# Weight conversions moved off GpSimd and spread over two stages, with branch hints, a shorter exit and two blocks of the last stage interleaved

## The chip, the cores and the metric

The kernel runs on one core of one Trainium2 chip. The metric is the time of one execution in device microseconds; before the change the median of 3 runs is 1045.09 us (1044.58 to 1046.73).

## The reference

Three layers follow each other. All inputs and outputs are arrays in float32 or wider, and the weights of the last layer arrive as pairs of 32-bit words (64-bit floats).

```python
q_pool = q.reshape(4, 8, 576, 2, 64).mean(axis=3)             # 1. attention with pooled queries
attn = softmax(q_pool @ k.T / 8) ; x = (attn @ v)              # x: 2304 tokens x 512
keep = (x @ w_skip) > 0                                        # 2. mixture of 8 experts, top 1
e = argmax(x[keep] @ w_gate) ; gate = max(softmax(x[keep] @ w_gate))
x[keep] += gate * (relu(x[keep] @ w1[e]) @ w2[e])              # w1: 8 x 512 x 1024, w2: 8 x 1024 x 512
h = x @ w_in                                                   # 3. dense layer, w_in: 512 x 2048
out = (h - tanh(h)) @ w_out                                    # w_out: 2048 x 512
```

## The kernel before

Four stages follow each other on the five engines. Each engine works through its own instructions in program order; the order is written out by hand.

**Attention** (0 to about 452 us) is not touched, but for one 256 KB store of zeros that moves to another queue. **Routing** (`Router.route`, `invert`, `gates`, `in_last`) is a chain of some 60 small operations on VectorE (DVE), with a few on ScalarE (ACT) and TensorE (PE). `route` counts the tokens of each expert, sorts the experts by size into `perm`, makes `more` (exit marks) and the slot of each token in `sg16`; `invert` turns slots into a list `inv` of token numbers. `Experts.load` on the GpSimd queue (POOL) needs `perm` to fetch the first expert's weights `w1f` and `w2f`; `fetch` gathers a tile of 128 tokens by `inv`.

**Experts** (`Experts.place`, `chain`, `tile`): the experts are run largest first. `place(a)` is entered if expert `a` has tokens; `chain(j)` nests one `If(n > j)` in another, one for each tile of 128 tokens. In these runs the experts have 5, 4, 1 and 1 tiles; I write (a, j) for tile j of expert a. A tile is: 96 matmuls `ps_bh` from the tokens `bxt` and the split weights `w1s` (12 for each of 8 columns f), a ReLU to `bhid` in two halves (ACT the high part, DVE the low part), four transposes of the next tokens, and 24 matmuls `ps_by` from `bhid` and `w2s`. The first tile of an expert also splits its weights into high and low halves (`split1`, `split2`: ACT, then DVE). When the last tile of an expert is done, the engines jump over the unused rest of its chain (line 945) into the next `place` (line 938).

**Weight conversions** (`Wide`): `w_in` and `w_out` are 16 jobs of 128 x 1024 values. A job loads 1 MB into one of two buffers `raw`, makes a float32 in `wa` by three DVE steps (lines 753, 755, 757), then a high part on ACT (line 776 or 779), for `w_in` also a scaled copy on ACT (line 777), and the low part on GpSimd (line 780). Jobs 0 to 13 run beside the experts' tiles (`SIDE`, two for a tile, called by `aside`), jobs 14 and 15 at the start of the last stage (`LATE`).

**Dense** (`Dense.run`, 644 us to the end): 9 blocks of 256 tokens in the order 0, 8, 1, 2, ... Each has 8 steps. A step runs `hid` (24 matmuls `ps_ch`, then an elementwise chain: ACT makes `u`, `t`, `z`, DVE makes `v` in five operations at lines 1089 to 1093, ACT rounds it to `gh`, GpSimd makes `gl`) and then `proj` of the step two before (12 matmuls `ps_co` with one eighth of `w_out`). `mix` and `transp` prepare the tokens of the next block: `mix` on DVE, `xs` high on ACT and low on DVE, and a transposing DMA to `xT`. Job 8 + u converts the eighth of `w_out` that step u uses.

Of the kernel before, what the change touches and what calls it, by code (L numbers as in the profile page):

```python
# [20 lines left out]
P = 128  # L21
# [458 lines left out]
NT = 18  # L480
# [9 lines left out]
class Router:  # L490
# [4 lines left out]
    def __init__(self, ctx, tc, w_skip, w_gate, x_all, ident32, ov):  # L495
# [9 lines left out]
        self.more, self.perm = t("more", [P, 2, E], I32), t("perm", [P, 3, E], I32)  # L505
        self.cnt, self.gate, self.last, self.least = t("cnt", [P, E]), t("gate", [P, NT]), t("last", [P, 1]), t("least", [P, E])
# [129 lines left out]
    def route(self, ps_pool, tag):  # L636
# [4 lines left out]
        for f in self.pick(e, NT):  # L641
# [4 lines left out]
        vals = T("vals", [P, 3, 1, E], I32)  # L646
        perm = T("permf", [P, 3, E])
        cmp, bt, mt, mm = T("cmp", S88), T("bt", S88), T("mt", S88), T("mm", [P, 3, E, E])
        few, last, so, sl = T("few", [P, 1]), self.last, T("so", [P, NT, E]), T("sl", [P, NT])
        iota8 = self.iota[:, 0, 0:E]  # L650
        nt = vals[:, 0, 0]
        V.tensor_copy(vals[:, 1, 0], iota8)
        V.tensor_tensor(out=n, in0=all_, in1=self.cnt, op=ALU.add)
        V.tensor_scalar(out=n1, in0=n, scalar1=float(P - 1), scalar2=None, op0=ALU.add)
        V.scalar_tensor_tensor(out=key, in0=n, scalar=float(E), in1=iota8, op0=ALU.mult, op1=ALU.subtract)
        V.tensor_scalar(out=nt, in0=n1, scalar1=7, scalar2=None, op0=ALU.logical_shift_right)
        V.tensor_tensor(out=cmp, in0=key.unsqueeze(1).to_broadcast(S88), in1=key.unsqueeze(2).to_broadcast(S88),
                        op=ALU.is_gt)
        V.tensor_tensor(out=bt, in0=cmp, in1=nt.unsqueeze(1).to_broadcast(S88), op=ALU.mult)
        V.tensor_reduce(out=rk, in_=cmp, axis=AX.X, op=ALU.add)  # L660
        V.tensor_reduce(out=base, in_=bt, axis=AX.X, op=ALU.add)
        V.tensor_tensor(out=mt, in0=rk.unsqueeze(1).to_broadcast(S88), in1=iota8.unsqueeze(2).to_broadcast(S88),
                        op=ALU.is_equal)
        V.tensor_copy(vals[:, 2, 0], base)
        V.tensor_tensor(out=mm, in0=vals.to_broadcast([P, 3, E, E]), in1=mt.unsqueeze(1).to_broadcast([P, 3, E, E]),
                        op=ALU.mult)
        V.tensor_reduce(out=perm, in_=mm, axis=AX.X, op=ALU.add)
        V.tensor_copy(self.perm, perm)
        V.tensor_reduce(out=last, in_=nt, axis=AX.X, op=ALU.add)
        V.tensor_tensor(out=perm[:, 1], in0=perm[:, 0], in1=self.least, op=ALU.is_lt)  # L670
        V.tensor_scalar(out=perm[:, 2, 0:E - 1], in0=perm[:, 0, 1:E], scalar1=0.0, scalar2=2.0 * NT,
                        op0=ALU.is_equal, op1=ALU.mult)
        V.tensor_reduce(out=few, in_=perm[:, 1], axis=AX.X, op=ALU.max)
        V.tensor_tensor(out=self.more[:, 1, 0:E - 1], in0=perm[:, 0, 0:E - 1], in1=perm[:, 2, 0:E - 1], op=ALU.add)
        V.tensor_scalar(out=last, in0=last, scalar1=1.0, scalar2=1.0, op0=ALU.max, op1=ALU.subtract)
        V.tensor_copy(self.more[:, 0, 1:2], few)
        V.tensor_copy(self.more[:, 0, 0:1], last)
        for f in self.rank(e, NT, before):
            f()
        for t in range(e, e + 3):  # L680
            self.row(t)
        V.tensor_tensor(out=so, in0=base.unsqueeze(1).to_broadcast([P, NT, E]), in1=self.oh, op=ALU.mult)
        V.tensor_reduce(out=sl, in_=so, axis=AX.X, op=ALU.add)
        V.tensor_tensor(out=self.r7[:, 1], in0=self.r7[:, 1], in1=sl, op=ALU.add)
        V.tensor_copy(self.sg16, self.r7[:, 1])
# [40 lines left out]
class Wide:  # L726
# [4 lines left out]
    def __init__(self, ctx, tc, w_in, w_out, wi, wo):  # L731
# [4 lines left out]
        self.jobs, self.open = [], []  # L736
# [23 lines left out]
    def run(self, i):  # L760
        for f in self.steps(i):
            f()
        self.open.append(i)

    def finish(self):
        for i in self.open:
            self.parts(i)
        self.open = []

    def parts(self, i):  # L770

        nc = self.nc
        _, dh, dl = self.jobs[i]
        a = self.a[i % 2].bitcast(F32)
        if dh.dtype == F16:
            nc.scalar.activation(dh, a, AF.Copy, scale=WS)
            nc.scalar.activation(a, a, AF.Copy, scale=WS)
        else:
            nc.scalar.copy(dh, a)
        nc.gpsimd.tensor_tensor(out=dl, in0=a, in1=dh if dh.dtype == F16 else dh.bitcast(F32), op=ALU.subtract)  # L780


class Experts:
# [7 lines left out]
    SIDE = {(0, 1): 2, (0, 2): 2, (0, 3): 2, (0, 4): 2, (1, 1): 2, (1, 2): 2, (1, 3): 2}  # L791
# [88 lines left out]
    def tile(self, a, j, base):  # L880
        nc = self.nc
        g = self.within(base + j)
        side = list(self.groups.get((a, j), ()))

        def aside():
            self.wide.finish()
            if side:
                self.wide.run(side.pop(0))
# [6 lines left out]
        aside()  # L895
        hs = []
        for f0 in (0, 4):
# [23 lines left out]
        aside()  # L921
        for f in range(8):
            mm(self.py, [t[:, f % 4] for t in hs[f // 4]], [t[:, f] for t in self.c2], f == 0, f == 7)
        if a + 1 < E:
            with self.tc.If(self.end <= j + 1):
                for f in range(self.PRE):
                    self.split1(f)
        if a + j:
            for i in self.groups.get((a, j + 1), ())[:2]:
                self.wide.load(i)  # L930

    def place(self, a):
# [5 lines left out]
        with tc.If(n > 0):  # L938
            T = mybir.EngineType
            if a + 1 < E:  # L940
                self.end = self.reg(self.more[:, 1], a, 3 * NT, (T.Activation, T.DVE))
            base = self.reg(self.perm[:, 2], a, CAP, (mybir.EngineType.Pool,))
            def chain(j):
                if j < self.MOST[a]:
                    with tc.If(n > j):
                        self.tile(a, j, base)
                        chain(j + 1)
            self.tile(a, 0, base)
            chain(1)
            self.place(a + 1)  # L950

    def run(self, before, after):
# [17 lines left out]
        self.place(0)  # L970
        before()
# [3 lines left out]
        with self.tc.If(few > 0):  # L975
            some = [self.reg(self.perm[:, 0], a, self.MOST[a], T) for a in range(2)]
            for (a, j), jobs in self.groups.items():
                with self.tc.If(some[a] <= j):
                    for i in jobs:
                        self.wide.load(i)  # L980
                        self.wide.run(i)
                    self.wide.finish()


class Dense:
# [3 lines left out]
    LATE = 2  # L989
# [9 lines left out]
    def setup(self, ctx, wide):  # L999
        tc, self.wide = self.tc, wide  # L1000
        self.late = []
        for i in range(len(wide.jobs) - self.LATE, len(wide.jobs)):
            wide.load(i)
            self.late += [*wide.steps(i), lambda i=i: wide.parts(i)]
# [42 lines left out]
    def transp(self, n, a):  # L1047
# [4 lines left out]
        if a == 0:  # L1052
            self.xs = self.xt.tile([P, 2, 2, DM], F16, tag="xs", name="xs")
            self.xT = self.xt.tile([P, 2, 2, 4, P], F16, tag="xT", name="xT")
# [76 lines left out]
    def run(self):  # L1131
# [11 lines left out]
        for i in range(NB):  # L1143
            for u in range(8):
                self.hid(self.ORDER[i], u, (i, u) == (NB - 1, 7))
                if len(self.q) > 2:
                    self.proj()
                for _ in range(2 if u == 0 else 1):
                    if self.late:
                        self.late.pop(0)()  # L1150
                if u in (2, 4):
                    self.mix(i + 1, u // 2 - 1)
                if u in (3, 5):
                    self.transp(i + 1, u // 2 - 1)
                if u == 7:
                    self.fetch(i + 2)
# [8 lines left out]
def pooled_attention__moe__tanhshrink_kernel(ctx, tc, q, k, v, moe_w_skip, moe_w_gate, moe_w1, moe_w2,  # L1165
# [8 lines left out]
    with tc.manual_schedule():  # L1174
# [7 lines left out]
        with ExitStack() as actx:  # L1182
# [5 lines left out]
            def on_pair(b, c):  # L1188
# [10 lines left out]
                if b == 0:  # L1199
                    for i in range(c, 6, 4):  # L1200
                        n = 5 if i < 5 else 1
                        todo.append(lambda i=i, n=n: nc.sync.dma_start(
                            out=ys[i * 5 * P:(i * 5 + n) * P].rearrange("(a p) d -> p a d", p=P),
                            in_=zero.unsqueeze(1).to_broadcast([P, n, DM])))
# [61 lines left out]
```

## Time and profile before

| quantity | value |
|---|---|
| median of 3 runs | 1045.09 us |
| the profiled execution's own time | 1046.08 us |
| its span, first to last instruction | 1044.6 us |
| busy: PE, DVE, ACT, POOL | 90%, 75%, 61%, 53% of the span |
| mean granted TensorE clock | 0.962 of full |

The profiled execution is 1.48 us longer than its span and 0.99 us longer than the median. A share of busy time is a mean over the four stages, so each stage is read for itself.

### The profile page before, as it was taken

The page shows a single profiled execution, that of the slowest core. Times are in us where ns is not written, and L with a number is a line of the kernel's source. Part 1 is how long each engine was busy: PE and PEld are TensorE (multiplying, and loading weights), DVE is VectorE, ACT ScalarE, POOL GpSimd, SP SyncE. Part 2 cuts the span into 40 slices and gives each one's busy share as a digit, 9 for nine tenths or more (in the row PEclk, how much of TensorE's full clock was granted, in tenths as well). Part 3 has the DMA queues.
Part 4 walks back from the last instruction along what each step waited for, and adds up shares of the span by engine and source line. Part 5 has one row for each costly group of instructions (what it writes and reads, how often), then busy time and mean ns, then how long its engine had stood idle before and what let it go on. Part 6 is the DMA issues. An engine that isn't in the chain of part 4 may idle for free. (4 is left out here: it accounts for less than half of the span.)

```text
span 1044.6 us, 25445 instructions
## 1 busy us (share of the span) xinstructions
PE 941.9 (90%) x10249; PEld 704.6 (67%) x10249; DVE 788.5 (75%) x1420; ACT 641.4 (61%) x1211; POOL 557.1 (53%) x491
## 2 busy tenths in 40 slices
PE   5689999999999999939878775999999999999998
PEld 2355666666666666637656543778888888888886
DVE  8678889888889998768979762867666666666654
ACT  4587999888999998835463451444444444444443
POOL 8847998888899986524646411342332223322221
PEclk8889999999999999969989887999999999999999
DMA  7765878666666720169657433121111211212100
GB/s 222 147 157 177 213 190 206 139 134 126 162 143 127 166 59 15 28 224 330 215 180 261 150 126 136 31 72 41 46 56 31 72 41 46 56 32 71 21 21 21
DMA packets 129796, 122.52 MB, mean 117 GB/s; under 512 B 92270, under 2 KB 96878, under 8 KB 128622
## 3 DMA queue, kind: packets, MB, share of 16 engines
q1 hardware_dynamic: 121934, 92.74, 34.7%
q0 software_dynamic: 7712, 27.79, 7.9%
q8 instruction: 92, 1.51, 0.6%
q14 instruction: 58, 0.48, 0.1%
HBM read 74.73 MB, written 19.14 MB: 90 GB/s over the span
## 5 line engine op out<-in xcount | busy, mean ns | idle before, releaser
L242 POOL TENSOR_TENSOR pl<-p,ph 128x512 f16<-128x512 f32 x214 | 263.8, 1252 | 59.5 <-ACT p L237 45.1
L188 DVE TENSOR_REDUCE m<-ps_m 128x1 f32<-128x384 f32 x432 | 225.5, 548 | 37.4 <-PE ps_m L187 34.7
L1095 POOL TENSOR_TENSOR gl<-v,gh 128x512 fp32r<-128x512 f32 x71 | 92.9, 1308 | 270.7 <-ACT gh L1094 268.3
L236 ACT ACTIVATE ph<-ps_e 128x512 f16<-128x512 f32 x279 | 177.0, 635 | 57.5 <-PE ps_e L248 54.2
L299 PEld LDWEIGHTS <-ph 128*128 128x128 f16 x2304 | 133.4, 99 | 49.7 <-issue 22.6
L1094 ACT CAST gh<-v 128x512 fp32r<-128x512 f32 x72 | 44.5, 619 | 188.5 <-DVE v L1093 188.5
L1078 PE MATMUL ps_ch<-xT,wi 128*128 128x256 f16 x576 | 158.7, 275 | 0.7 <-ACT xT L1062 0.7
L1079 PE MATMUL ps_ch<-xT,wi 128*128 128x256 f16 x576 | 157.9, 274 | 1.1 <-DMA xT<-xs 0.8
L1080 PE MATMUL ps_ch<-xT,wi 128*128 128x256 f16 x576 | 157.9, 274 | 0.0
L187 PE MATMUL ps_m<-ks,qT 128*128 128x384 f16 (+1 forms) x480 | 122.7, 338 | 23.9 <-DVE m L188 16.1
L299 PE MATMUL ps_a<-vh,ph 128*128 128x65 f16 x1152 | 136.7, 195 | 0.0
L299 PE MATMUL ps_a<-vh,pl 128*128 128x65 f16 x1152 | 136.6, 195 | 0.0
L299 PE MATMUL ps_a<-vl,ph 128*128 128x65 f16 x1152 | 136.5, 195 | 0.0
L1089 DVE SCALAR_TENSOR_TENSOR v<-u,ps_ch 128x512 f32<-128x512 f32 x72 | 49.3, 685 | 114.4 <-ACT t L1087 108.9
L237 ACT ACTIVATE p<-ps_e 128x512 f32<-128x512 f32 x211 | 134.5, 637 | 0.0
L1111 PE MATMUL ps_co<-wo,gh 128*128 128x512 f32 x288 | 119.7, 416 | 0.0
L1113 PE MATMUL ps_co<-wo,gl 128*128 128x512 f32 x288 | 113.7, 395 | 1.5 <-POOL gl L1095 1.5
L247 PE MATMUL ps_e<-qT,ks 128*128 128x512 f16 x288 | 111.4, 387 | 2.6 <-DVE pl L242 1.8
L1112 PE MATMUL ps_co<-wo,gh 128*128 128x512 f32 x288 | 113.5, 394 | 0.0
L248 PE MATMUL ps_e<-qT,kh 65*128 65x512 f16 x288 | 111.8, 388 | 1.9 <-DMA qT<-mt 1.9
L299 PEld LDWEIGHTS <-pl 128*128 128x128 f16 x1152 | 108.4, 98 | 0.0
L187 PEld LDWEIGHTS <-qT 128*128 128x128 f16 (+1 forms) x480 | 42.9, 102 | 68.1 <-issue 34.3
(222 smaller groups left out, 2152.8 us busy)
## 6 DMA issues: line engine op xcount, KB each, us to landing
v<-in_v_dram SPq DMA_DIRECT2D x16, 576.0 KB
k<-in_k_dram SPq DMA_DIRECT2D x15, 576.0 KB
q<-in_q_dram SPq DMA_DIRECT2D x16, 512.0 KB
raw<-in_moe_w_in_dram SPq DMA_DIRECT2D x8, 1024.0 KB
w1f<-in_moe_w_dram POOLq DMA_DIRECT2D x8, 1024.0 KB, 7.6
w2f<-in_moe_w_dram POOLq DMA_DIRECT2D x8, 1024.0 KB, 8.3
raw<-in_moe_w_out_dram SPq DMA_DIRECT2D x8, 1024.0 KB
ys<-zero SPq DMA_DIRECT2D x5, 1280.0 KB
```

The costliest lines, as they stand in the source:

```text
L187: nc.tensor.matmul(ps[o, 0:384], w, ks[:, h, c * 384:(c + 1) * 384], start=True, stop=True)
L188: nc.vector.tensor_reduce(out=s["m2"][:, i, c:c + 1], in_=ps[:, 0:384], axis=AX.X, op=ALU.max)
L236: nc.scalar.activation(ph, ps, AF.Exp, scale=2.0 ** -20)
L237: nc.scalar.activation(src, ps, AF.Exp, scale=2.0 ** -20)
L242: (nc.vector if dve else nc.gpsimd).tensor_tensor(out=pl, in0=src, in1=ph, op=ALU.subtract)
L299: self.nc.tensor.matmul(o, x, r, start=first and i == 0, stop=k == NKT - 1 and i == 2, skip_group_check=True)
L1078: nc.tensor.matmul(ps[:, a], self.wi[0][:, w], xh[:, c], start=c == 0, stop=False)
L1079: nc.tensor.matmul(ps[:, a], self.wi[0][:, w], xl[:, c], start=False, stop=False)
L1080: nc.tensor.matmul(ps[:, a], self.wi[1][:, w], xh[:, c], start=False, stop=c == 3)
L1111: nc.tensor.matmul(o, gh[:, a, s], self.wo[0][:, w], start=f == 0, stop=False)
L1112: nc.tensor.matmul(o, gh[:, a, s], self.wo[1][:, w], start=False, stop=False)
L1113: nc.tensor.matmul(o, gl[:, a, s], self.wo[0][:, w], start=False, stop=f == 15)
```

## The change

- Routing: the small operations of `route` are interleaved instead of run one group after the other, and the eight that make `more` move into `tails`, called after `invert`.
- Hints: each tile marks, on all five engines, whether the branch to its next tile will be taken; the jump out of the routing's `few` case is marked too.
- Exit: the register `end` is loaded on all engines, and after the first tile of an expert one test of it skips the rest of the chain and all later experts.
- Conversions: the low part moves from GpSimd to DVE, the scaled copy of `w_in` goes away, and the steps of a tile's jobs are handed out one by one: 3 at the tile's start, 2 between its halves, the rest behind its last matmuls and behind the next expert's first splits.
- Five jobs (11 to 15) instead of two run in the last stage, whose first two blocks are interleaved; the second block's tokens are prepared in steps 1 and 2.
- The 256 KB store of zeros moves from the SyncE queue to the GpSimd queue.

```diff
-        nc.gpsimd.tensor_tensor(out=dl, in0=a, in1=dh if dh.dtype == F16 else dh.bitcast(F32), op=ALU.subtract)
+        half = dh.dtype == F16
+        return (
+            lambda: nc.scalar.activation(dh, a, AF.Copy, scale=WS if half else 1.0),
+            lambda: nc.vector.scalar_tensor_tensor(out=dl, in0=a, scalar=WS, in1=dh, op0=ALU.mult, op1=ALU.subtract)
+            if half else nc.vector.tensor_tensor(out=dl, in0=a, in1=dh.bitcast(F32), op=ALU.subtract))
+
+    def queue(self, jobs, load=()):
+        out, low = [], None
+        for i in jobs:
+            s, (hi, lo) = list(self.steps(i)), self.parts(i)
+            if low:
+                h, l = low
+                s[0] = lambda f=s[0], h=h: (h(), f())
+                s.insert(1, l)
+            if i + 2 in load:
+                s[-1] = lambda f=s[-1], i=i: (f(), self.load(i + 2))
+            out += s
+            low = hi, lo
+        return out + ([lambda: (low[0](), low[1]())] if low else [])
...
-    SIDE = {(0, 1): 2, (0, 2): 2, (0, 3): 2, (0, 4): 2, (1, 1): 2, (1, 2): 2, (1, 3): 2}
+    SIDE = {(0, 1): 2, (0, 2): 2, (0, 3): 2, (0, 4): 1, (1, 1): 2, (1, 2): 1, (1, 3): 1}
...
+        if j + 1 < self.MOST[a]:
+            self.tc.mark_branch_hint_location("t%d_%d" % (a, j + 1), hint=n > j + 1, engines=ALL)
...
-        aside()
+        aside(3)
...
-                aside()
+                aside(2)
...
-        aside()
         for f in range(8):
             mm(self.py, [t[:, f % 4] for t in hs[f // 4]], [t[:, f] for t in self.c2], f == 0, f == 7)
         if a + 1 < E:
             with self.tc.If(self.end <= j + 1):
                 for f in range(self.PRE):
                     self.split1(f)
+        aside(len(side))
...
-                self.end = self.reg(self.more[:, 1], a, 3 * NT, (T.Activation, T.DVE))
+                self.end = self.reg(self.more[:, 1], a, 3 * NT, ALL)
...
-                    with tc.If(n > j):
-                        self.tile(a, j, base)
+                    with tc.If(n > j, label="t%d_%d" % (a, j)):
+                        self.tile(a, j, base, n)
...
-            chain(1)
-            self.place(a + 1)
+            with tc.If(self.end != 2 * NT + 1) if a + 1 < E else ExitStack():
+                chain(1)
+                self.place(a + 1)
...
-    LATE = 2
+    LATE = 5
+    TWICE = (5, 6, 7, 8)
...
+        halves = [(n, u) for u0 in (0, 4) for n in range(2) for u in range(u0, u0 + 4)]
+        steps = halves[:8] + sorted(halves[8:], key=lambda s: (s[1], s[0])) + [(n, u) for n in range(2, NB) for u in range(8)]
+        side = {1: (1, 0), 2: (1, 1), 9: (2, 0), 11: (2, 1)}
+        for s, (n, u) in enumerate(steps):
+            self.hid(self.ORDER[n], u, s == len(steps) - 1)
+            if len(self.q) > 2:
+                self.proj()
+            for _ in range(2 if s in self.TWICE else 1):
+                if self.late:
+                    self.late.pop(0)()
+            if s in side:
+                self.mix(*side[s])
+                self.transp(*side[s])
```

## Rows read from the trace of the kernel before

**Rows 1.** Stretches: length, PE, PEld, DVE, ACT, POOL busy (count), PEclk, DMA share, GB/s.
```profile
469.70:627.20 157.50, 131.24 (x1363) 97.08 (x1361) 127.48 (x137) 77.04 (x126) 72.36 (x58) 0.92 0.61 210
644.10:687.10 43.00, 40.47 (x265) 32.26 (x265) 32.18 (x46) 18.13 (x32) 13.82 (x10) 0.95 0.28 98
687.10:1044.60 357.50, 352.94 (x2327) 289.02 (x2326) 225.49 (x363) 161.90 (x284) 99.09 (x80) 1.00 0.16 44
```
**Rows 2.** PE's waits, 470 to 645 us: total us, times, longest us.
```profile
PE ps_by L889 <- DVE bhid L905: 8.9, 7, 1.8
PE ps_i L1041 <- ACTq L975: 8.3, 1, 8.3
```
**Rows 3.** PE's timeline in the expert stage: start, us, work [idle before <-releaser].
```profile
482.89 5.52 PE L889 MATMUL ps_bh<-bxt,w1s 128*128 128x128 f16 x96
492.89 2.33 PE L889 MATMUL ps_by<-w2s,bhid 128*128 128x512 f16 x10 [1.01 <-DVE bhid L905]
...
537.18 8.26 PE L889 MATMUL ps_bh<-bxt,w1s 128*128 128x128 f16 x96 [4.58 <-ACTq L945]
...
593.80 7.29 PE L889 MATMUL ps_bh<-bxt,w1s 128*128 128x128 f16 x96 [5.33 <-DVE w1s L851]
...
612.05 0.90 PE L889 MATMUL ps_bh<-bxt,w1s 128*128 128x128 f16 x7 [5.33 <-PEq L945]
615.11 6.50 PE L889 MATMUL ps_bh<-bxt,w1s 128*128 128x128 f16 x89 [2.16 <-issue]
```
**Rows 4.** Stretch behind the first jump: length, PE busy (count), PEclk, DMA share, GB/s.
```profile
537.20:542.90 5.70, 5.70 (x54) 0.50 0.18 22
```
**Rows 5.** Instructions of single lines: duration min/median/max in ns, first and last start.
```profile
L757 DVE SCALAR_TENSOR_TENSOR wa<-raw,wa x14: 1224/2128/3257, 484.3 to 582.2; 128x1024 uint32<-128x1024 uint32 x14
L780 POOL TENSOR_TENSOR wi<-wa,wi x8: 2117/2130/3197, 489.0 to 531.9; 128x1024 f16<-128x1024 f32 x8
L779 ACT CAST wo<-wa x8: 1041/1045/1068, 554.8 to 686.5; 128x1024 fp32r<-128x1024 f32 x8
L1034 DVE SCALAR_TENSOR_TENSOR cx<-cy,gate,cx x18: 735/742/1762, 639.9 to 976.2; 128x512 f32<-128x512 f32 x18
```
**Rows 6.** DVE's timeline around the end of tile (0, 1).
```profile
489.04 3.19 DVE L757 SCALAR_TENSOR_TENSOR wa<-raw,wa 128x1024 uint32<-128x1024 uint32 x1
...
499.31 0.68 DVE L753 TENSOR_SCALAR wa<-raw 128x1024 uint32<-128x1024 uint32 x1
```
**Rows 7.** Timelines of DVE, POOL and PE in the routing.
```profile
456.55 0.18 DVE L668 CAST perm<-permf 128x24 int32<-128x24 f32 x1
...
459.72 0.18 DVE L685 CAST sg<-r 128x18 f16<-128x18 f32 x1
...
458.61 0.97 POOL L836 DMA_DIRECT2D w1f<-in_moe_w_dram  x1 [13.70 <-DVE kf L608]
...
467.04 1.09 PE L865 MATMUL ps_bt<-ident,bx 128*128 128x128 f32 x4 [2.10 <-DMA bx<-xd,inv]
```
**Rows 8.** Chain that ended last, early in the dense stage: start, us, what.
```profile
682.97 4.14 DMA xT<-xs
...
687.41 0.11 PE ps_ch L1080
...
689.82 0.23 PE ps_co L1111
```
**Rows 9.** DVE's timeline in the dense stage.
```profile
681.43 1.51 DVE L1063 SCALAR_TENSOR_TENSOR xs<-cx,xs 128x512 f16<-128x512 f32 x1 [0.17 <-ACT xs L1062]
...
693.67 0.69 DVE L1089 SCALAR_TENSOR_TENSOR v<-u,ps_ch 128x512 f32<-128x512 f32 x1 [1.78 <-ACT t L1087]
...
698.46 0.69 DVE L1089 SCALAR_TENSOR_TENSOR v<-u,ps_ch 128x512 f32<-128x512 f32 x1 [1.78 <-ACT t L1087]
```
**Rows 10.** PE's waits, 645 us to the end: total us, times, longest us.
```profile
PE ps_co L1113 <- POOL gl L1095: 1.5, 1, 1.5
PE ps_ch L1079 <- DMA xT<-xs: 0.8, 1, 0.8
```

More of the change, by code (lines that the diff above doesn't have):

```diff
@@ new lines, in route, with tails @@
+        V.tensor_copy(vals[:, 1, 0], iota8)
+        rank = self.rank(e, NT, before)
+        for i, f in enumerate(place):
+            f()
+            if i < len(rank):
+                rank[i]()
+        for f in rank[len(place):]:
+            f()
+        for t in range(e, e + 3):
+            self.row(t)
+        for i, f in enumerate(slots):
+            f()
+            if i < len(order):
+                order[i]()
+    def tails(self):
+        V, vals, perm, few, last = self.nc.vector, self.vals, self.permf, self.few, self.last
+        V.tensor_reduce(out=last, in_=vals[:, 0, 0], axis=AX.X, op=ALU.add)
@@ L672, in route @@
                         op0=ALU.is_equal, op1=ALU.mult)
+        V.tensor_scalar(out=last, in0=last, scalar1=1.0, scalar2=1.0, op0=ALU.max, op1=ALU.subtract)
         V.tensor_reduce(out=few, in_=perm[:, 1], axis=AX.X, op=ALU.max)
         V.tensor_tensor(out=self.more[:, 1, 0:E - 1], in0=perm[:, 0, 0:E - 1], in1=perm[:, 2, 0:E - 1], op=ALU.add)
-        V.tensor_scalar(out=last, in0=last, scalar1=1.0, scalar2=1.0, op0=ALU.max, op1=ALU.subtract)
+        V.tensor_copy(self.more[:, 0, 0:1], last)
         V.tensor_copy(self.more[:, 0, 1:2], few)
[L677 to L685, printed above, removed]
     def invert(self, ps_pool):
@@ L774, in parts, with run @@
         a = self.a[i % 2].bitcast(F32)
[L775 to L779, printed above, removed]
-        nc.gpsimd.tensor_tensor(out=dl, in0=a, in1=dh if dh.dtype == F16 else dh.bitcast(F32), op=ALU.subtract)
+        half = dh.dtype == F16
[16 more added lines that the diff above has]
+        return out + ([lambda: (low[0](), low[1]())] if low else [])
+    def run(self, jobs):
+        for f in self.queue(jobs):
+            f()
+ALL = tuple(getattr(mybir.EngineType, n) for n in ("PE", "Activation", "Pool", "DVE", "SP"))
 class Experts:
@@ L970, in run @@
         self.place(0)
+        self.tc.mark_branch_hint_location("few", hint=few, engines=T)
         before()
@@ L1000, in setup @@
         tc, self.wide = self.tc, wide
-        self.late = []
-        for i in range(len(wide.jobs) - self.LATE, len(wide.jobs)):
+        jobs = range(len(wide.jobs) - self.LATE, len(wide.jobs))
+        for i in jobs[:2]:
             wide.load(i)
-            self.late += [*wide.steps(i), lambda i=i: wide.parts(i)]
+        self.late = wide.queue(jobs, jobs[2:])
         pool = lambda n, b: ctx.enter_context(tc.tile_pool(name=n, bufs=b))
@@ L1142, in run @@
             self.transp(0, a)
[L1143 to L1156, printed above, removed]
+        halves = [(n, u) for u0 in (0, 4) for n in range(2) for u in range(u0, u0 + 4)]
[11 more added lines that the diff above has]
+                self.transp(*side[s])
+            if n > 1 and u in (2, 4):
+                self.mix(n + 1, u // 2 - 1)
+            if n > 1 and u in (3, 5):
+                self.transp(n + 1, u // 2 - 1)
+            if s == 4:
+                self.fetch(2)
+            if n and u == 7:
+                self.fetch(n + 2)
         while self.q:
@@ L1211, in pooled_attention__moe__tanhshrink_kernel @@
             att.run()
+            nc.gpsimd.dma_start(out=ys[25 * P:26 * P], in_=zero)
             router.route(att.ps_mx, "mx")
```

86 lines of the change are left out of this document (41 added, 45 removed).

## Prediction

> **What bounds the kernel now.** I read the stretches first, then PE's waits, then PE's own timeline. The stretches [rows 1] show two cases. From 687 us on PE is busy 352.94 of 357.50 us at full clock: every microsecond put in PE's way there is lost, and none can be won. In the expert stage PE is busy 131 of 157.5 us at a mean clock of 0.92: that is where time can be won. The waits say in which form. Seven times, 8.9 us together, PE's second product waits for the low half of `bhid`, which DVE makes [rows 2]. Three times PE stands still for 4.58, 5.33 and 5.33 us between the last tile of one expert and the first of the next, and once more for 2.16 us inside the first tile of expert 3 with no releaser shown [rows 3]. At the exit it stands still 8.3 us [rows 2]. What follows each jump is slow as well: 96 matmuls take 5.52 us in an undisturbed tile but 8.26, 7.29 and 0.90 + 6.50 us behind the jumps [rows 3], and the granted clock there is 0.50, the lower level, 1.2 GHz, after 4.6 us in which PE did nothing [rows 4].
>
> **The change part by part, as time of the profiled execution.**
>
> *Conversions without GpSimd.* A two-input DVE step on 128x1024 takes 1.22 us alone and up to 3.26 us when it meets the GpSimd subtraction of 2.12 us [rows 5]; tile (0, 1) shows 3.19 us for line 757, with `bhid` queued behind it [rows 6]. The change takes this meeting away and adds one DVE operation to each job, which the trace of before doesn't have: below, a 128x512 operation (0.69), above, a blocked one (3.26). It has two inputs and 1024 columns as line 757, so I take 1.22. A tile with two jobs then costs DVE 2 x (0.7 + 1.22 + 1.22 + 1.22) = 8.7 for the jobs, 2.1 for two halves of `bhid` and one of `bxt`, and about 1.3 for the wait of the last low part for ACT: 12.1 us. The tile on PE: from 482.89 to about 495.1 it lasts 12.2, less 1.0 of waiting, so 11.1 [rows 3]. DVE falls back by 1.0 per such tile, but the order puts the low `bhid` early. Working forward from (0, 1): DVE is 1.6 late at (0, 2), 2.5 at (0, 3), 3.3 at (0, 4). `bhid` is late there by 0.2 and 0.9 us, elsewhere not. The reload of a buffer stays hidden: freed at 492.2 in (0, 1), read at 499.31 without a wait [rows 6], and now needed 6 us after it comes free; if that doesn't hold, 1 to 2 us in two tiles. Term: -8.9 + 1.1 = **-7.8** (-4 to -9).
>
> *Hints.* The excess of the three jumps over back-to-back tiles is 15.24 of idle time, 2.16 inside and 6.39 of slow clock: 23.8 us [rows 3]. If the marked target is there in time, what is left is the branch itself, the new load of `end` on PE with the tile's matmuls queued behind it, and the hint's own register work. No row prices these on PE; the first splits of the next expert are ready by then, because the change puts the rest of the conversions behind them. Bounds: nothing, while the queued `ps_by` matmuls run, or the full 4.6 to 5.3. I take 0.8 each, 2.4. Idle times of 1.0 to 1.8 us [rows 2] left the clock alone, so the slow clock goes too. Two things come back: tile (3, 0) arrives 5 us earlier against its `w2f`, which is issued late in (2, 0), about 1.7 us; and the 2.16 inside a tile happened in one jump of three, 0.7. Term: -23.8 + 2.4 + 1.7 + 0.7 = **-19.0** (0 to -23).
>
> The jumps are the code at the target not being there. The Trainium skill, "Runtime: NRT & Kernel Launch", section "Instruction fetch mechanics", says that prefetch is purely sequential and that a taken branch out of the window forces a fetch of its target before execution goes on; taken alone, this speaks against the hints, and by it the term would be 0. The trace of before holds no hint and can't decide it.
>
> *Exit.* Today two jumps in a row, 8.3 us [rows 2]; after it one, not marked, as long as the mean of the three, 5.1 [rows 3]. Term: **-3.2** (0 to -5). Behind it the gathers, the last store and the first transposes come in the same order.
>
> *Routing.* Of two chains, one gets shorter: `sg16`, ready at 459.9, comes 2.0 earlier, since some 20 dependent operations of 0.2 us fill each other's gaps. The other gets longer: `perm` now ends beside `sg16`, about 457.6 instead of 456.7, so the first `w1f` is issued 0.9 later, and the gather behind it on POOL's queue 1.5 earlier, not 2.0. PE's transposes waited last for that gather [rows 7], but ACT does two splits of `w1f` before it can copy the transposes. One earlier, one later: **0** (-0.7 to +0.9). The eight moved operations are about 1 us on DVE behind `inv`, under the gather's flight of 4 to 5 us. The store of zeros goes to a queue that is idle then; it is not needed before the stage's end: 0, and at most its own issue, about 1 us.
>
> *The last stage.* Here PE pays. A `hid` is 24 matmuls of 0.11 us, 2.64; a `proj` 12 of 0.23, 2.8 [rows 8]. The elementwise loop between ACT and DVE takes 698.46 - 693.67 = 4.79 us per step, 1.78 of it idle on DVE [rows 9]. Count from the first `v`, at 650.5. Step 1 starts at 4.8; five operations (3.0), a conversion step (1.22), `mix` (0.74 [rows 5]), and ACT's `xs` (0.6) come before ACT's `u` and `t` (1.1) for step 2, which starts at 11.4. Step 2 has the same in its way; the low `xs` of the second block is ready at 17.6, or 18.4 if it stretches to 1.51 as in [rows 9]. The transposing DMA took 4.14 until PE went on [rows 8], so the block's tokens arrive at 22.2. The 1 MB load of job 13 is issued just ahead of it on SyncE's queue; that may add up to 3.
>
> PE is ready much earlier. Its first `hid` ran at the slow clock (5.3 us), two more at the full one end at 4.1; then 1.5 of waiting [rows 10], `proj`, `hid`, `proj`: 13.8. Its next instruction is `hid` of the second block, with all other matmuls queued behind it: **+8.5** (+5 to +11). After such an idle time the clock goes down; 1.8 to 2.7 us were lost behind the jumps, here I take half of the upper end, **+1.3** (0 to 2.7). At step 16 `proj` needs job 15's eighth of `w_out`, which ACT (1.04 [rows 5]) and DVE (1.22) finish behind the chain of step 15: **+1.6** (0 to 4). Between steps 5 and 15 the loop lengthens to 5.4 on average (21 us of conversions, of which 1.78 a step fit the idle time) against PE's 5.42 a step; GpSimd's `gl` still meets two-input operations, so I add **+1.0** (0 to 15, see the rivals). The 0.8 us wait for the first `xT` goes [rows 10]: **-0.8**. Term: **+11.6** (+4 to +16).
>
> Sum: -7.8 - 19.0 - 3.2 + 0 + 11.6 = -18.4. The span becomes 1026.2; the profiled execution has 1.48 around its span and stands 0.99 above the median of the runs shown, so the median comes to 1027.
>
> **The rivals.**
>
> *The hints bring nothing.* The mark is set at a tile's start, some 250 PE instructions ahead of its branch; if the fetch of those in between displaces the target, or no target is fetched, the three jumps stay, and tile (3, 0) doesn't outrun its weights: -7.8 - 3.2 + 11.6 = +0.6, **1046**. For it: nothing in the profile has shown a jump being covered. Against it: PE's jump is known a full 11 us ahead, over twice the longest gap. If the hints help ACT and DVE alone, PE's gaps stay and it comes to the same.
>
> *DVE against GpSimd in the last stage (the other side).* With `gl` on GpSimd and 15 more two-input operations on DVE in the first 16 steps, each meeting can hold DVE about 1.0 us: `mix` goes from 0.74 to 1.76 [rows 5]. If it happens in nearly every step, up to 15 us lengthen a loop that already equals PE's, and PE waits for each. Alone this gives 1027 + 14 = 1041; it makes the kernel slower once more than 20 us go that way, that is 1.3 a step, or together with hints that bring nothing, 1046 + 14 = **1060**. Against it: DVE's idle time per step is where `gl` lies today.
>
> *The last stage costs little.* If the second block's tokens come sooner, because DVE's early steps wait less than the loop says, the stall is 3 instead of 8.5 and the clock stays up: 1027 - 6.8 = **1020**. For it: one undisturbed `xs` and a DMA without traffic save 1.5. Against it: the chain of five operations, conversion step, `mix` and `xs` in step 2 can't be shorter.
>
> **How the numbers follow.** The forecast, hints that work and a paid start of the last stage, has 0.62; its own range, from the ends of hints and of the last stage, is 1017 to 1036. Hints that bring nothing: 0.18. The port rival to the point of being slower: 0.08. The cheap last stage: 0.12. Differences under 0.2% (2.1 us) can't be told from none here. Faster by more: 0.62 + 0.12 + a third of the 0.18 (the conversions' gain at its upper end, the last stage at its lower): 0.80. Within: half of the 0.18: 0.09. Slower: the rest of it and the port rival: 0.11. The range takes in the cheap last stage and part of the way to the jumps that stay: 1010 to 1043.
>
> **What would show it.** Right: PE's waits for `bhid` under 2 us in sum; the gaps ahead of tiles (1, 0), (2, 0), (3, 0) near 1 us and the clock at 1.00 behind them; line 757 at 1.22 us throughout; one gap of about 5 us at the exit; one PE wait of 8 to 9 us for `xT` some 20 us into the last stage. Wrong: gaps of 5 us between experts, DVE steps of over 2 us in the last stage's first 16 steps, or many small PE waits for `gl` there. The likeliest way to be wrong is the hint, then the size of the stall for `xT`.

## The result, and the profile after

The changed kernel takes 1035.31 us (median of 5 runs, 1031.25 to 1036.44) against 1045.09 us; the ratio is 0.9898, with a 95% interval of 0.9871 to 0.9925. It is faster, by 10 us where 18 were forecast. The profiled execution has a span of 1029.8 us, 14.8 less than that of before; attention, which is not touched, gives 3.4 of these and differs by as much from run to run.

The stretches of the changed kernel: expert stage, first 43 us of the last stage, the rest (columns as in [rows 1]):

```profile
465.90:600.70 134.80, 124.63 (x1363) 92.04 (x1362) 105.84 (x139) 65.73 (x115) 33.80 (x44) 0.96 0.64 222
613.10:656.10 43.00, 32.79 (x201) 25.22 (x201) 26.98 (x40) 15.16 (x26) 11.01 (x9) 0.81 0.40 126
656.10:1029.80 373.70, 365.51 (x2394) 298.18 (x2391) 246.50 (x384) 168.31 (x292) 99.27 (x79) 0.99 0.18 47
```

The expert stage is 22.7 us shorter than in [rows 1]; the first 43 us of the last stage hold 32.8 us of PE's work instead of 40.5, at a mean clock of 0.81. PE's waits, 470 to 645 us and then to the end, say where:

```profile
PE ps_ch L1108 <- DMA xT<-xs: 9.3, 1, 9.3
PE ps_bh L917 <- ACT w1s L877: 7.7, 1, 7.7
PE ps_i L1071 <- ACTq L1005: 4.5, 1, 4.5
...
PE ps_by L917 <- DVE bhid L933: 0.3, 1, 0.3
...
PE ps_co L1141 <- ACT wo L783: 3.1, 1, 3.1
PE ps_co L1142 <- DVE wo L785: 1.0, 1, 1.0
```

The 8.9 us for `bhid` and the 8.3 us at the exit [rows 2] are 0.3 and 4.5 now. New are 9.3 us for the second block's tokens and 4.1 us for job 15's eighth of `w_out`. The 7.7 us stand at one place, which PE's timeline shows beside the other two entries of a new expert; then the clock behind it (columns as in [rows 3] and [rows 4]):

```profile
523.73 5.52 PE L917 MATMUL ps_bh<-bxt,w1s 128*128 128x128 f16 x96 [1.09 <-ACTq L973]
568.91 5.52 PE L917 MATMUL ps_bh<-bxt,w1s 128*128 128x128 f16 x96 [1.07 <-PEq L973]
587.78 7.28 PE L917 MATMUL ps_bh<-bxt,w1s 128*128 128x128 f16 x96 [7.73 <-ACT w1s L877]
```
```profile
584.50:591.40 6.90, 3.62 (x35) 3.65 (x36) 3.10 (x5) 2.71 (x5) 0.00 (x0) 0.51 0.46 173
635.70:646.00 10.30, 3.50 (x16) 2.35 (x17) 6.55 (x9) 4.00 (x7) 2.78 (x2) 0.51 0.63 178
717.70:721.10 3.40, 3.40 (x9) 2.59 (x9) 3.30 (x6) 0.55 (x1) 1.46 (x2) 0.52 0.52 117
```

Two entries out of three are as forecast: 1.1 us, then 5.52 us for 96 matmuls. The third, into tile (3, 0) behind the one-tile expert 2, costs more than before. There the changed kernel executes no mark, though each tile was meant to have one (e2). The clock is at its lower level (0.51) three times: there, in the wait for `xT`, and at job 15.

For the stages as a whole I took three points of PE's timeline in each profiled execution: the first `ps_bh`, the end of the last `ps_by` (where the wait for `ps_i` begins), and the first `hid` matmul. In us, with the exit being that wait:

| kernel | ratio to before, interval | median | experts | exit | dense |
|---|---|---|---|---|---|
| before | 1 | 1045.1 | 158.4 | 8.3 | 400.5 |
| the change | 0.9898 (0.9871 to 0.9925) | 1035.3 | 135.5 | 4.5 | 416.7 |
| e1 no marks | 0.9932 (0.9906 to 0.9959) | 1036.9 | 138.7 | 3.5 | 417.9 |
| e2 no exit test | 0.9947 (0.9926 to 0.9968) | 1039.0 | 135.8 | 9.8 | 416.7 |
| e3 old last stage | 0.9836 (0.9807 to 0.9865) | 1026.5 | 147.2 | 4.4 | 399.3 |
| e4 early tokens | 0.9896 (0.9870 to 0.9923) | 1033.1 | 135.9 | 4.4 | 416.0 |
| e5 marks on before | 0.9932 (0.9912 to 0.9952) | 1036.5 | 150.2 | 8.1 | 399.6 |
| e7 low part on GpSimd | 0.9937 (0.9919 to 0.9955) | 1036.5 | 137.4 | 5.1 | 418.4 |
| e8 six steps | 0.9809 (0.9790 to 0.9828) | 1024.4 | 137.2 | 4.3 | 407.5 |
| e9 e3 with GpSimd | 0.9838 (0.9813 to 0.9862) | 1026.3 | 147.1 | 4.5 | 399.0 |
| e10 late exit test | 0.9817 (0.9793 to 0.9840) | 1024.8 | 133.5 | 6.8 | 406.0 |
| e11 store by ACT | 0.9761 (0.9739 to 0.9784) | 1020.0 | 131.9 | 4.4 | 406.9 |

Each ratio has its own runs of before, so kernels are compared by ratios and not by medians; 0.001 is 1.04 us. The intervals of e1 and e7 overlap that of the change, so what is said of these two rests on their traces.

Beside the work of the engines, the traces record each branch instruction of their sequencers (`COMPARE_BRANCH`) with start and duration; the views shown here leave them out. I call PE's branch out of an expert's last tile its jump. PE comes to it while its last matmuls still run.

### The profile page after: what moved, and what is told of

Its sections match the earlier page's. It is cut to its first block, busy times and chain, and to the rows that moved or that the text cites. A ratio compares the mean times of both kernels' runs of the same rounds, so it can differ in the third digit from the quotient of the medians.

```text
span 1029.8 us, 25570 instructions
## 1 busy us (share of the span) xinstructions
PE 937.1 (91%) x10249; PEld 700.1 (68%) x10249; DVE 780.3 (76%) x1436; ACT 633.4 (62%) x1203; POOL 517.3 (50%) x476
## 5 line engine op out<-in xcount | busy, mean ns | idle before, releaser
L299 PE MATMUL ps_a<-vh,pl 128*128 128x65 f16 x1152 | 135.9, 195 | 0.0
L299 PE MATMUL ps_a<-vh,ph 128*128 128x65 f16 x1152 | 135.9, 195 | 0.0
```

The lines of the kernel that those rows point to most:

```text
L299: self.nc.tensor.matmul(o, x, r, start=first and i == 0, stop=k == NKT - 1 and i == 2, skip_group_check=True)
```

## Experiments

**e1: no marks.** The edit:

```diff
-        if j + 1 < self.MOST[a]:
-            self.tc.mark_branch_hint_location("t%d_%d" % (a, j + 1), hint=n > j + 1, engines=ALL)
```

> The changed kernel without the marks at the tiles' starts (that of the few case stays). Theory, the marks bring the next expert's code in time: the gaps ahead of tiles (1, 0) and (2, 0) go from 1.09 and 1.07 us back to about 5, the slow clock behind them comes back (96 matmuls in 7 to 8.3 us instead of 5.5), the gap ahead of (3, 0) stays at 7 to 8; the expert stage grows from 134.8 to about 146 to 149 us and the time by 11 to 14 us, to about 1047. Rival, the marks do nothing and the gaps shrank because of the new order of the conversions: gaps and time stay as they are (1035).

PE's timeline at the three entries without marks:

```profile
526.35 7.15 PE L915 MATMUL ps_bh<-bxt,w1s 128*128 128x128 f16 x96 [2.93 <-ACT w1s L877]
573.28 5.52 PE L915 MATMUL ps_bh<-bxt,w1s 128*128 128x128 f16 x96 [1.22 <-ACT w1s L877]
591.23 2.08 PE L915 MATMUL ps_bh<-bxt,w1s 128*128 128x128 f16 x18 [6.81 <-PEq L971]
```

Both theories fail. The marks are worth 3.2 us of the stage here, 1.84 in the first gap and 1.63 in its slow clock; but most of what came off the gaps of 4.58 and 5.33 [rows 3] stays off without any mark. Something else in the change shortened them. By the traces, PE's jumps at these two entries last 3.99 and 3.84 us in e1; in the kernel before they last 6.06 and 3.50, the second with another stop of 3.37 us ahead of PE's next branch. And at (2, 0) in e1 PE comes to its jump 3.66 us before its last matmul ends, 2.27 us in the kernel before, so that less of it shows. Why unmarked jumps differ so in length stays open.

**e3: the last stage as before.** Two jobs in it instead of five, so that the last tiles (0, 4) and (1, 3) have two jobs again:

```diff
-    SIDE = {(0, 1): 2, (0, 2): 2, (0, 3): 2, (0, 4): 1, (1, 1): 2, (1, 2): 1, (1, 3): 1}
+    SIDE = {(0, 1): 2, (0, 2): 2, (0, 3): 2, (0, 4): 2, (1, 1): 2, (1, 2): 2, (1, 3): 2}
...
-    LATE = 5
-    TWICE = (5, 6, 7, 8)
+    LATE = 2
+    TWICE = (0,)
...
-        steps = halves[:8] + sorted(halves[8:], key=lambda s: (s[1], s[0])) + [...]
+        steps = [(n, u) for n in range(NB) for u in range(8)]
...
```

> The changed kernel with the last stage as before: two conversion jobs in it, 14 beside the tiles, blocks one after the other. Theory, the new last stage costs the 16.2 us by which it is longer in the profiles: the dense stage goes from 416.7 to about 400 to 402 us, no wait for xT over 1.5 us; in the expert stage the three tiles with a job more cost DVE 1 to 4 us in all; time -10 to -15, so 1020 to 1025. Rival, without GpSimd the tiles can't carry 14 jobs: the waits for bhid and the late tiles take 10 us or more there, and the time stays within 3 us of 1035.

6 us faster than the change, by two large amounts of opposite sign: the dense stage gives 17.4 back, the expert stage takes 11.7. The latter is what I had priced at 1 to 4. The end of tile (0, 4) on DVE, on ACT, and PE's entry into (1, 0):

```profile
523.80 1.22 DVE L771 SCALAR_TENSOR_TENSOR wa<-raw,wa 128x1024 uint32<-128x1024 uint32 x1
525.05 1.23 DVE L773 SCALAR_TENSOR_TENSOR wa<-raw,wa 128x1024 uint32<-128x1024 uint32 x1
527.40 1.22 DVE L784 SCALAR_TENSOR_TENSOR wi<-wa,wi 128x1024 f16<-128x1024 f32 x1 [1.12 <-ACTq L973]
```
```profile
526.31 1.06 ACT L783 ACTIVATE wi<-wa 128x1024 f16<-128x1024 f32 x1 [4.16 <-DVE wa L773]
528.22 2.71 ACT L877 ACTIVATE w1s<-w1f 128x512 f16<-128x512 f32 x5 [0.85 <-ACTq L973]
```
```profile
528.83 7.15 PE L917 MATMUL ps_bh<-bxt,w1s 128*128 128x128 f16 x96 [4.71 <-DVEq L973]
...
579.39 5.82 PE L917 MATMUL ps_bh<-bxt,w1s 128*128 128x128 f16 x65 [4.71 <-DVEq L973]
```

PE is done at 528.83 - 4.71 = 524.12. DVE, with all marks in place, ends its second job's last operation at 528.62, and PE starts 0.2 us later, released by DVE's sequencer at the branch. So the engines meet at the entry of a new expert: PE goes on when the last of PE, ACT and DVE has reached its branch. In the changed kernel, with one job in a last tile, ACT and DVE are done at 520.7 and 522.4, ahead of PE's 522.6.

In the kernel before DVE is late as well, but there it is not what holds PE. DVE's last splits ahead of the first entry, and ACT's first work behind it:

```profile
532.34 3.41 DVE L851 SCALAR_TENSOR_TENSOR w1s<-w1f,w1s 128x512 f16<-128x512 f32 x3 [1.53 <-ACT w1s L850]
```
```profile
537.90 2.71 ACT L850 ACTIVATE w1s<-w1f 128x512 f16<-128x512 f32 x5 [4.55 <-ACTq L945]
```

DVE's splits end at 535.75, 3.15 us after PE was done (537.18 - 4.58 = 532.60 in [rows 3]). But PE's own jump runs from 530.31 to 536.37, and ACT, idle since 533.35, is behind its own at 537.11, 0.07 us before PE starts. At the second entry DVE is done at 590.95, and PE's two branches only at 593.50. So two things lie side by side in the kernel before: the jump, which is the longer one, and late engines, which the jump hides. To take away one of the two leaves the other: the marks alone leave the late engine (e3), the changed kernel without marks keeps the jump (e1, 2.93 us of gap at (1, 0)).

**e5: the marks alone, on the kernel before.**

```diff
+        if j + 1 < self.MOST[a]:
+            self.tc.mark_branch_hint_location("t%d_%d" % (a, j + 1), hint=n > j + 1, engines=ALL)
...
-                    with tc.If(n > j):
+                    with tc.If(n > j, label="t%d_%d" % (a, j)):
```

> The kernel before with nothing but the marks at the tiles' starts. The prediction's step, the marks bring the next expert's code in time: the gaps of 4.58, 5.33 and 5.33 us go to about 1, the clock behind them stays up, the expert stage falls by 13 to 19 us and the time to 1026 to 1032. Rival from the first four runs, the gap is what ACT and DVE, which reach their own branch late behind the last tile's second conversion job, need to get to the next expert: here ACT and DVE end after PE, so the marks shorten each gap by 1 us at most but for the one-tile expert; the time falls by 1 to 5 us, to 1040 to 1044.

PE's timeline at the three entries:

```profile
534.62 5.57 PE L894 MATMUL ps_bh<-bxt,w1s 128*128 128x128 f16 x72 [4.38 <-ACTq L950]
587.56 7.15 PE L894 MATMUL ps_bh<-bxt,w1s 128*128 128x128 f16 x96 [2.48 <-DVEq L950]
601.61 5.52 PE L894 MATMUL ps_bh<-bxt,w1s 128*128 128x128 f16 x96 [1.28 <-DVEq L950]
```

The stage falls by 8.2 us and the time by 0.0068, 7 us: between the two theories. PE's own jumps shrink to 0.39, 0.36 and 0.46 us, but the first gap hardly moves: ACT's jump is not covered.

```profile
535.51 2.71 ACT L853 ACTIVATE w1s<-w1f 128x512 f16<-128x512 f32 x5 [4.52 <-ACTq L950]
```

ACT's sequencer is behind its branch at 534.56, 0.06 us before PE starts; DVE had been done since 533.38. At the second entry, where the gap is halved, DVE is last, as the rival says: it ends at 587.36, and PE starts 0.2 us later. The third gap, 5.33 us in [rows 3] where ACT and DVE had long been idle, falls to 1.28 with the clock up behind it. A mark does cover a jump of PE; it can't cover an engine that comes late.

**e2: no exit test.** Why did the mark not cover the third entry in the changed kernel?

```diff
-            with tc.If(self.end != 2 * NT + 1) if a + 1 < E else ExitStack():
-                chain(1)
-                self.place(a + 1)
+            chain(1)
+            self.place(a + 1)
```

> The changed kernel without the test of end behind an expert's first tile, so that a chain is left as before the change. H1, that unmarked test stands between the mark and the marked branch in a one-tile expert and loses the mark: the gap ahead of tile (3, 0) falls from 7.73 to about 1 us, its 96 matmuls from 7.28 to 5.5, together -7 to -9 us; the exit gets a second jump, +0 to +4; the time about -4 to -8, so 1027 to 1031. H2, the jump from expert 2 to 3 has another cause: its gap stays at 7 to 8 us, and the exit costs up to 4 more: 1035 to 1039.

PE's timeline around tile (3, 0), and the first three of ACT's waits from 560 to 605 us:

```profile
587.74 4.01 PE L917 MATMUL ps_bh<-bxt,w1s 128*128 128x128 f16 x69 [1.53 <-ACT w1s L877]
592.65 1.68 PE L917 MATMUL ps_bh<-bxt,w1s 128*128 128x128 f16 x27 [0.90 <-issue]
596.90 0.63 PE L892 MATMUL ps_bt<-ident,bx 128*128 128x128 f32 x4 [2.57 <-DMA bx<-xd,bix]
```
```profile
ACT bhid L932 <- PE ps_bh L917: 7.8, 2, 7.2
ACT by L896 <- DMA ys<-by: 5.6, 1, 5.6
ACT w1s L877 <- PEq L973: 3.1, 1, 3.1
```

H1 is right on the gap: without the test between mark and branch it is 1.53 us, 0.90 follow inside, and the clock stays up (69 matmuls in 4.01 us). The traces show how the test does it. A mark is an instruction of its own (`BRANCH_PREFETCH_HINT`). PE executes 11 of them in e2, one in every tile. In the changed kernel it executes 7, and none in the first tile of any expert, and tile (2, 0) is the first and last of its expert. In e10 and e11 it executes 10: the missing one is that of (3, 0), the only tile there that the exit test follows. So the test doesn't use up a mark; where it follows, the program holds none. Why the mark is left out isn't shown. The two branches of line 952 stand between mark and jump in every tile and do no harm.

PE's jumps at the three entries, in us:

| kernel | (1, 0) | (2, 0) | (3, 0) |
|---|---|---|---|
| before, no marks | 6.06 | 3.50, then a stop of 3.37 | 5.90 |
| e1, no marks | 3.99 | 3.84 | 6.45 |
| the change, no mark for (3, 0) | 0.38 | 0.35 | 7.42 |
| e3, no mark for (3, 0) | 0.38 | 0.35 | 6.86 |
| e5, all marked | 0.39 | 0.36 | 0.46 |
| e2, all marked | 0.38 | 0.35 | 0.35 |

H1's time is not right: the kernel is 0.0049, 5 us, slower than the change, and the stage is as long as with the 7.73 us. The tile that now comes early waits for something that the gap had hidden: ACT can't evacuate `by` until it hears that the store of the tile before, on GpSimd's queue, is done. The weights ahead of the store on that queue are not the whole of it. In e10, which waits in the same way, the store landed 7.3 us after its issue, at 585.7, and ACT went on at 593.66. Each time ACT starts just behind a step of GpSimd's sequencer at its own branch (`INC_SWDGE_SEM`; it ends at 596.71 in e2, ACT starts at 596.83). Ahead of that step GpSimd waits until 595.73, and the last packets of its queue, those of `w2f`, end at 595.26. That this step is what releases ACT is read from the order in time, at four places in e2 and e10; no run tests it alone.

At the exit PE has two branches again, 0.40 us for the marked one and 4.67 for the other. Last there is once more GpSimd's step, which ends at 614.43; ACT starts at 614.59, and the exit takes 9.8 us instead of 4.5.

**e4: the second block's tokens a step earlier.**

```diff
-        side = {1: (1, 0), 2: (1, 1), 9: (2, 0), 11: (2, 1)}
+        side = {0: (1, 0), 1: (1, 1), 9: (2, 0), 11: (2, 1)}
```

> The changed kernel with the second block's mix and transposition in steps 0 and 1 instead of 1 and 2. Theory, the wait for xT is as long as the chain of steps 1 and 2 ahead of it: it falls from 9.3 to 2 to 4 us, the clock stays up behind it, and the time falls by 6 to 9 us, to 1026 to 1029; the first steps' v come later by 1 to 2 us, which PE's first wait may show. Rival, the transfer itself is late (the 1 MB load ahead of it on the same queue, or tokens not yet gathered): the wait stays over 7 us and the time within 2 us of 1035.

PE's waits, 613 to 730 us:

```profile
PE ps_co L1142 <- DVE wo L785: 4.4, 2, 3.4
PE ps_co L1141 <- ACT wo L783: 2.9, 1, 2.9
PE ps_co L1143 <- POOL gl L1125: 1.2, 2, 0.8
PE ps_ch L1108 <- DMA xT<-xs: 1.1, 1, 1.1
PE ps_co L1141 <- ACT gh L1124: 1.1, 1, 1.1
PE ps_ch L1109 <- DMA xT<-xs: 1.0, 1, 1.0
```

The wait for `xT` falls from 9.3 to 2.1, as the theory says, and the time stays, as the rival says. 3.4 us come up for the low part of job 11's eighth, which the stall had hidden; of the dense stage's 416.7 only 0.7 us are gone. The stall was the first symptom of 16 steps in which DVE and ACT have more to do than PE. DVE's first `v` behind the stall and the one 12 steps later, in the changed kernel:

```profile
648.32 0.69 DVE L1119 SCALAR_TENSOR_TENSOR v<-u,ps_ch 128x512 f32<-128x512 f32 x1 [5.00 <-ACT t L1117]
717.31 0.69 DVE L1119 SCALAR_TENSOR_TENSOR v<-u,ps_ch 128x512 f32<-128x512 f32 x1
```

That is 5.75 us a step, where PE needs 5.42.

**e7: the low part of the eleven jobs beside the tiles back on GpSimd.**

```diff
+        if i < 11:
+            def hi():
+                nc.scalar.activation(dh, a, AF.Copy, scale=WS if half else 1.0)
+                if half:
+                    nc.scalar.activation(a, a, AF.Copy, scale=WS)
+            return hi, lambda: nc.gpsimd.tensor_tensor(out=dl, in0=a, in1=dh if half else dh.bitcast(F32), op=ALU.subtract)
```

> The changed kernel with the low part of the eleven jobs beside the tiles back on GpSimd (and ACT's scaled copy for w_in); the last stage's five jobs stay as they are. The conversions' step of the prediction, -7.8: DVE's blocked two-input steps come back at 2 to 3 us each, PE waits again for bhid, the expert stage grows by 4 to 8 us, time 1039 to 1043. Rival, DVE gives up 1.22 us a job and that pays for the blocked steps: the stage stays within 2 us, and what made the waits for bhid vanish is the order of the steps within a tile: 1033 to 1037.

The third DVE step of a job, 466 to 606 us (shapes, count, busy us, mean ns, idle), in the changed kernel and then in e7; and two of e7's PE waits, 462 us to the end:

```profile
L773 DVE SCALAR_TENSOR_TENSOR wa<-raw,wa 128x1024 uint32<-128x1024 uint32 x11 | 13.5, 1225 | 0.4
```
```profile
L773 DVE SCALAR_TENSOR_TENSOR wa<-raw,wa 128x1024 uint32<-128x1024 uint32 x11 | 15.4, 1404 | 0.4
```
```profile
PE ps_bt L898 <- DMA bx<-xd,bix: 2.0, 3, 1.2
PE ps_by L923 <- DVE w2s L884: 0.6, 2, 0.4
```

The rival is nearer: the stage grows by 1.9 us (the ratio by 0.0039, 4 us, part of which is a wait for `xT` of 11.3 us instead of 9.3), and no wait for `bhid` comes back. The blocked step appears (1404 ns on average against 1225, 2175 in the kernel before), but it no longer stands in `bhid`'s way. What PE waits for is a gather that GpSimd issues later.

**e9: e3 with the low part of the last tiles' jobs on GpSimd** (the edit of e7 with `i in (6, 7, 12, 13)`).

> The kernel with the last stage as before (e3) and the low part of the four jobs of the last tiles (0, 4) and (1, 3) on GpSimd (with ACT's scaled copy for the two of w_in). Theory, the gap between experts is what DVE and ACT are late at their branch by: DVE ends its last tile 2 to 3 us sooner, the gaps of 4.7 us at (1, 0) and (2, 0) fall to 1 to 3 and the slow clock behind them goes with those under 2: the expert stage falls from 147 to 139 to 143, time 1019 to 1023. Rival, GpSimd's subtraction blocks DVE's two-input steps for as long as it takes work off: gaps as they are, 1025 to 1029.

A miss: 0.9838 against e3's 0.9836. ACT's last operation ahead of the branch and PE's entry into (1, 0):

```profile
527.99 1.06 ACT L786 ACTIVATE wa<-wa 128x1024 f32<-128x1024 f32 x1
```
```profile
529.14 6.83 PE L923 MATMUL ps_bh<-bxt,w1s 128*128 128x128 f16 x96 [5.03 <-ACTq L979]
```

DVE is free earlier, but ACT, which makes the high part and the scaled copy behind DVE's third step, ends at 529.05, and PE starts 0.09 us later. Another engine is the last one, and the gap is the same.

**e8: twelve jobs beside the tiles, none second in a last tile; four in the last stage, six steps of a block at a time.**

```diff
-    SIDE = {..., (0, 4): 1, (1, 1): 2, (1, 2): 1, (1, 3): 1}
+    SIDE = {..., (0, 4): 1, (1, 1): 2, (1, 2): 2, (1, 3): 1}
...
-    LATE = 5
-    TWICE = (5, 6, 7, 8)
+    LATE = 4
+    TWICE = (0, 2, 4)
...
-        halves = [(n, u) for u0 in (0, 4) for n in range(2) for u in range(u0, u0 + 4)]
+        halves = [(n, u) for n in range(2) for u in range(6)] + [(n, u) for u in (6, 7) for n in range(2)]
...
-        side = {1: (1, 0), 2: (1, 1), 9: (2, 0), 11: (2, 1)}
+        side = {1: (1, 0), 3: (1, 1), 9: (2, 0), 11: (2, 1)}
```

> The changed kernel with 12 jobs beside the tiles (the second one goes to tile (1, 2), which is not an expert's last), four in the last stage, and its first two blocks in the order six steps of the first, six of the second, then by turns; the second block's tokens in steps 1 and 3. Theory, what the last stage loses is DVE's and ACT's extra work ahead of step 16 and the early need for xT: the wait for xT falls under 2 us, the dense stage goes from 416.7 to 404 to 409; the expert stage grows by 0 to 2 us, since a job that isn't in a last tile delays no branch; time 1024 to 1029. Rival, the wait only moves to the eighths of w_out and the loop stays as long: dense 412 or more, time 1031 to 1036.

Both stages as expected: dense 9.2 us shorter than the change's, experts 1.7 longer, the gaps at (1, 0) and (2, 0) still 1.1. PE's largest waits from 610 us to the end:

```profile
PE ps_co L1143 <- POOL gl L1125: 2.6, 6, 0.6
...
PE ps_ch L1108 <- DVE v L1119: 1.1, 1, 1.1
PE ps_ch L1109 <- DMA xT<-xs: 1.0, 1, 1.0
```

**e10 and e11: the exit test only from the fourth expert on, and then the stores of `by` on ACT's queue,** both on e8. For its stores ACT also loads two registers that only GpSimd loaded.

```diff
-            with tc.If(self.end != 2 * NT + 1) if a + 1 < E else ExitStack():
+            with tc.If(self.end != 2 * NT + 1) if 3 <= a < E - 1 else ExitStack():
```
```diff
-        nc.gpsimd.dma_start(out=self.ys[ds(self.within(g) * P, P), :], in_=self.y)
+        nc.scalar.dma_start(out=self.ys[ds(self.within(g) * P, P), :], in_=self.y)
```

> The kernel with six steps (e8), with the exit test only behind the first tile of the fourth and later experts, so that none stands between the mark and the branch of the one-tile expert 2, and the exit behind expert 3 keeps its one jump. H1, an unmarked test between mark and branch loses the mark: the gap ahead of (3, 0) goes from 6.58 to 1.0 to 1.6 us and its 96 matmuls from 7.88 to 5.5, the exit stays at 4.3 to 5.1; but the store of by behind the next weights on GpSimd's queue then holds tile (3, 0) by some 5 us as in e2, so the time falls by 2 to 5 us only, to 1019 to 1022. H2, the gap has another cause (the weights' transfers fill the DMA engines then, and the code comes late with or without a mark): gap 5 us or more, time 1022 to 1026.

> As e10, with the stores of by on ACT's queue instead of GpSimd's. If ACT's wait of 5 to 6 us in tile (3, 0) is the store queued behind 3 MB of weights on GpSimd's queue, it goes, and the time falls by 3 to 6 us against e10, unless w2f is late too: then PE or ACT waits there for w2f, 0 to 3 us of the gain left. Rival, the store is late because the DMA engines are full, whatever its queue: the wait stays over 4 us and the time within 2 us of e10.

PE's entry into (3, 0) in e10, ACT's longest wait of e10 from 560 to 640 us, and PE's entry in e11:

```profile
586.39 5.60 PE L917 MATMUL ps_bh<-bxt,w1s 128*128 128x128 f16 x96 [1.53 <-DVEq L973]
```
```profile
ACT by L896 <- DMA ys<-by: 11.6, 2, 7.9
```
```profile
586.46 5.52 PE L917 MATMUL ps_bh<-bxt,w1s 128*128 128x128 f16 x96 [1.83 <-DVEq L973]
```

In e10 H1 has the gap right once more, and the exit has one jump, but the time is that of e8 (0.9817 and 0.9809): ACT waits 11.6 us for the end of two stores, part of it in the exit, which grows to 6.8. Both stores had landed long before, at 585.7 and 602.2. ACT goes on at 593.66 and 607.25, and GpSimd's step at its branch ends at 593.56 and 607.08. In e11 ACT doesn't wait for a store at all; it is 0.0056, 6 us, faster than e10, and at 0.9761 the fastest kernel here, 14 us ahead of the change. PE there waits for neither `w2f` nor the gather in tile (3, 0). The gain is as e11's expectation has it, but its reason, a store queued behind the weights, accounts for 7.3 of the 15.3 us between the store's issue and ACT's going on in e10.

## Why the prediction came out as it did

The time lies in the range, 8 us above the value, with two large terms off by 7 and 5 us the same way. By the steps:

- **Conversions, -7.8.** The waits for `bhid` fell by 8.6 and tiles lie 11.0 us apart, so the size is right. The reason is half right: e7 shows 1.9 us for taking the subtraction off GpSimd. It isn't the three jobs fewer either: with all 14 beside the tiles (e3) PE's wait for `bhid` is 0.3 us as well. That leaves the order of the steps within a tile, which every run of the new conversions keeps and none tests alone.
- **Hints, -19.0.** The rows after against [rows 3] give 3.49 and 4.26 us of gaps and 2.74 and 1.77 of slow clock at the first two entries, and at the third 2.40 lost in the gap, 2.16 won inside the tile and 0.12 in the matmuls: -12.1 in all. This is the step that came out worst. "The jumps are the code at the target not being there", and a mark covers them, is borne out for PE at every marked entry: 0.35 to 0.46 us against 3.5 to 7.4 unmarked. What the term had wrong is, first, that each entry has a mark: with the exit test, which I priced as a gain only, the third has none, and its gap of 7.73 instead of 0.8 alone is as much as the difference. Second, it put late engines at nothing. With the marks in place a second conversion job in the last tile still costs 4.7 us at each of the first two entries (e3). That these two came out as forecast owes as much to that job's going, which I had booked as a cost in the last stage and as nothing here. So the marks alone are worth 8.2 us of the stage on the kernel before (e5) and 3.2 in the changed one (e1), and the forecast of the first two gaps was right in part by luck.
- **The rule on fetching.** The third entry is the cleanest jump: 5.33 us of gap in [rows 3], 6.81 without marks (e1), 7.73 in the changed kernel, where its mark is missing, 1.28 and 1.53 with a mark (e5, e2). The Trainium skill, "Runtime: NRT & Kernel Launch", section "Instruction fetch mechanics", has the jump right, a taken branch that forces a fetch of its target before execution can go on; that prefetch is purely sequential does not hold here for a marked branch. The traces agree with the first: 16 KB packets of the instruction queue start inside PE's unmarked jumps (at 607.13 before, at 584.48 in the changed kernel), and none inside the marked one of e2 (585.57 to 585.92).
- **Exit, -3.2:** -3.8 (8.3 to 4.5). **Routing, 0:** -0.3 by the same points of PE's timeline.
- **Last stage, +11.6:** +16.2. The chain for `xT` was worked out rightly, 9.3 for 8.5. Mis-sized were job 15 (4.1 for 1.6) and the slow clock (1.3): behind the first stall 16 matmuls came 0.21 us apart instead of 0.11, 1.7, and behind job 15 11 of them took 4.2 us instead of 2.6, 1.6 more. With the 0.8 of [rows 10] that went and 0.8 less waiting for `gl` these make 15.1 of the 16.2. The port rival is real in single rows, `mix` at 1.75 us and line 773 at 2.2 beside `gl`, 5 such steps in the first 16, and did not decide. What I had not seen is that the stall for `xT` hid other late work (e4): its removal alone gives nothing.

As a trade, moving three jobs from the tiles to the last stage cost 17.4 us there and gained 11.7 here (e3); e8 has most of both.

## What to carry to other kernels

Where engines meet at a branch, read first who arrives last: a mark shortens the branch, and only less work ahead of it helps the late engine. Count in the trace the marks that were executed: a test put behind a tile took its mark out of the program. And before a stall is removed, look for what else would be late in its place: a stall for `xT` hid a conversion, a jump hid a late DVE, and a gap hid ACT's wait for GpSimd.

## What the runs showed of the hardware that was not expected

- In every run PE's jump into a new expert lasted 0.35 to 0.46 us where a mark was executed ahead of it, and 3.5 to 7.4 us where none was. In e4, e7, e8 and e9, which have no mark for (3, 0), that jump took 5.2 to 7.0 us.
- A store of 256 KB on GpSimd's queue landed 7.3 us after its issue in e10, behind 2 MB of weights, and ACT, which waited for it, went on another 8.0 us later, 0.10 us after a step of GpSimd's sequencer at a branch (592.61 to 593.56). With the store on ACT's own queue nothing waited for it (e11).
- With the mark in place ACT still took 4.52 us over its branch at the first entry in e5 (from 530.99 to 535.51), and it was ACT that PE waited for; in e3 ACT took 0.85 us. Why a mark serves ACT at one entry and not at another was not settled.
- Behind a gap of 2.48 us (e5) the 96 matmuls took 7.15 us, at a granted clock of 0.67 from 587.6 to 591.0; behind one of 1.83 us (e11) they took 5.52 at 1.00.
